# A linear-attention and feed-forward kernel: GpSimd's queue, not ScalarE's, asks for the load of w

## The chip, the core and the metric

The kernel runs on one core of a Trainium2 chip. The metric is the device time of one execution in microseconds (us); less is better. A core has five engines with a queue of instructions each: PE (TensorE, matrix products), DVE (VectorE), ACT (ScalarE), POOL (GpSimd) and SP (SyncE). In this kernel SP computes nothing: it issues DMAs, the transfers between the device's memory and the on-chip memory, and waits. "ACTq" or "SPq" in a profile is such an issue on that engine's queue.

## The reference

The first part is a linear attention with a decaying state, for 4 batches, 8 heads, 768 steps and a head size of 48. The second part is a feed-forward block with a gated softmax and a normalisation, from 384 to 1024 and back, over 3072 rows.

```python
for t in range(S):
    kt, vt, rt = (k[:, :, t], v[:, :, t], r[:, :, t])
    cur = np.einsum('bhd,bhe->bhde', u[None] * kt, vt)
    y[:, :, t] = np.einsum('bhd,bhde->bhe', rt, state + cur)
    state = w[None, :, :, None] * state + np.einsum('bhd,bhe->bhde', kt, vt)
...
h = x @ w_in
sm = e / (np.sum(e, axis=-1, keepdims=True) + 1e-09)
solu = h * sm
ln = (solu - mu) / np.sqrt(var + 1e-06) * g_ln
return (ln @ w_out).astype(np.float32)
```

Here `x` is y with its heads side by side, and `e` is exp(h - max h). w is small: 8 heads by 48 numbers, 1.5 KB. Each number is the decay of one row of the state.

## The kernel before

The 768 steps are cut into 6 chunks of 128 for each of the 4 batches: 24 units of (batch, chunk), chunk by chunk, so that a batch's next unit comes four units later. A unit's scores are computed as a product of decayed r and decayed k, and the state is carried from chunk to chunk inside the tiles that hold v. Behind each unit's attention follows its share of the feed-forward block: a product with w_in (L951), exponential and normalisation, and a product with w_out (L1061, L1106). The units overlap: a unit's second product comes several units behind its attention.

The order is written out by hand. `manual_schedule` (L459) keeps each engine's instructions in the order of the code, so an instruction that waits holds back everything behind it on its engine. A second path, `general_path`, runs only when a check on the data at the end asks for it, and it isn't taken here.

The start is what the change touches:

- ACT's queue issues two loads: w into `wq` (L493), then u into one row of `u_bc` (L496). ACT's first table load waits for u.
- SP's queue issues k and r of unit 0 (L475), the first piece of w_in (L524), k and r of unit 1, v of unit 0 (L480), the second piece of w_in, and so on (L594 to L608). Loads share eight semaphores in turn, so from the second piece of w_in on, each load is issued only after the load that last used its semaphore has landed.
- DVE clears the padding of `wq`, of five k tiles and five r tiles (L494 to L499), two banks of PSUM (L504), and sets one column of the table `tab` (L634).
- POOL makes `ident`, the identity for transposes, by `make_identity` (L611), a row of ones (L613), clears padding of the six v tiles (L623), and makes the masks (L671 to L676) and `ones` (L710).
- PE runs three products on `ident` whose result isn't used (`spin(3)`, L621), then transposes `wq` into `wd_ps` (L636), then spreads u over 128 partitions (`u_ps`, L638).

Then DVE clips `wd_ps` into `pw` (L643) and makes the powers of w by repeated squaring (L648, L649), and from them `tab` (L654), which doubles its filled part at each of seven steps. PE turns the table into `kdec` (L664). POOL computes `wide` from it (L1200), then `rku`, the product of k, u and r (L734, L735), and `kp`, the decayed k (L721). DVE sums rku to `own` (L739), ACT writes own on the diagonal of the score tile (L749), DVE copies the scores over it (L827), and PE makes unit 0's y (L858). The later units repeat this.

```python
wq = const.tile([HP, 2, P], F32, name="wq")
...
nc.tensor.transpose(wd_ps, wq.rearrange("a q d -> a (q d)"), ident[0:HP, 0:HP])
...
nc.gpsimd.tensor_tensor(out=wide.rearrange("p (a q) -> p a q", q=2)[P : P + D, :, q],
                        in0=back[rows, :, 0], in1=pw[rows, 0, 0], op=ALU.mult)
```

HP is 4, P is 64. In `wq` a row holds two heads of 48 numbers, each padded to 64.

Of the kernel before, what the change touches and what calls it, by code (L numbers as in the profile page):

```python
# [399 lines left out]
def direct_path(  # L400
# [29 lines left out]
    nc = tc.nc  # L430
    B, H, S, D = r.shape
# [53 lines left out]
    wq = const.tile([HP, 2, P], F32, name="wq")  # L485
# [4 lines left out]
    w_out_sb = const.tile([128, KF, dm], F32, name="w_out_sb")  # L490
    decays = const.tile([128, HP], F32, name="decays")

    nc.scalar.dma_start(out=wq[:, :, 0:D], in_=w.rearrange("(a q) d -> a q d", q=2))  # L493
    nc.vector.memset(wq[:, :, D:], 1.0)  # L494
    u_row = u_bc[0:1].rearrange("p h d -> p (h d)")
    nc.scalar.dma_start(out=u_row, in_=u.rearrange("h d -> (h d)").unsqueeze(0))  # L496
# [143 lines left out]
    for vt in vts:  # L640
        nc.scalar.activation(out=vt[:, 1].rearrange("p h x -> p (h x)"),
                             in_=ident[:, 0:1].to_broadcast([128, H * P]), func=ACT.Copy, scale=0.0)
# [916 lines left out]
def kernel(tc: tile.TileContext, *args):  # L1559

    with tc.tile_pool(name="flag", bufs=1) as pool:
        bad = direct_path(tc, pool, *args)
        value = tc.nc.values_load(bad, min_val=0, max_val=1)
        with tc.If(value != 0):
            general_path(tc, *args)
# [30 lines left out]
```

## Time and profile before

| what | value |
|---|---|
| median of 3 runs | 325.61 us (325.03 to 327.12) |
| the profiled execution: its own time | 326.14 us |
| its span, first to last instruction | 324.4 us |
| mean granted TensorE clock | 0.998 |
| w's issue on ACT's queue | starts 0.79 us, takes 1.25 us |
| u's issue on ACT's queue | starts 2.08 us, takes 0.27 us |
| wd_ps, the transpose of w | starts 4.34 us |
| first rku on POOL | starts 8.42 us |

Times in the profile count from the start of the span. Durations below come from the one profiled execution. The page gives each engine's busy time and the chain of work that ended last, followed back from the last instruction. The view of waits says which engine stood still, and what ended that. The timeline lists instructions in order of time; a bracket gives the idle time before one, and what released it. The DMA view counts packets by queue: queue 1 is SP's, queue 10 is ACT's.

### The profile page before, as it was taken

The numbers are of one execution on the slowest core, as the hardware profiler recorded it, in microseconds if no ns is written. First come the engines' busy times: TensorE is split into PE (matmuls) and PEld (weight loads), VectorE is DVE, ScalarE is ACT, GpSimd is POOL, SyncE is SP. The second block draws the span as 40 slices with busy tenths as digits, with TensorE's granted clock in tenths as the row PEclk, the third lists the DMA queues.
The fourth block names the chain that finished last, engine by engine and source line by source line (L and its number), as shares of the span: only waits on it lengthen the run. The fifth ranks groups of instructions, "written<-read, shape, count | busy, mean of one in ns | idle before, by whom it ended". The sixth has DMA issues, their size and how long they took to land.

```text
span 324.4 us, 9658 instructions
## 1 busy us (share of the span) xinstructions
PE 310.6 (96%) x3909; PEld 216.8 (67%) x3909; DVE 254.2 (78%) x434; ACT 244.0 (75%) x414; POOL 219.8 (68%) x237
## 2 busy tenths in 40 slices
PE   6889999999999999999999999999999999999993
PEld 4766565555556457668678668668668667769992
DVE  7796999998887979999779678997579675385471
ACT  4875888888469888868968969959958949957420
POOL 3989778799999999999999999979044020131000
PEclk9999999999999999999999999999999999999999
DMA  8999999579999999986998999987893473674611
GB/s 166 244 257 210 205 225 184 79 140 156 192 168 173 179 173 146 165 176 114 169 204 169 182 209 183 212 207 102 190 186 67 100 180 86 143 164 87 178 61 61
DMA packets 165780, 52.64 MB, mean 162 GB/s; under 512 B 158301, under 2 KB 161502, under 8 KB 165726
## 3 DMA queue, kind: packets, MB, share of 16 engines
q1 hardware_dynamic: 165712, 51.92, 83.0%
q8 instruction: 33, 0.54, 0.7%
q14 instruction: 21, 0.17, 0.2%
q10 hardware_dynamic: 14, 0.00, 0.0%
HBM read 26.75 MB, written 4.72 MB: 97 GB/s over the span
## 4 chain that ended last, share of the span: by engine, by line
PE 61%; POOL 14%; DVE 10%; issue 6%; ACT 4%; DMA 3%; POOLq 0%; DVEq 0%; ACTq 0%
PE h_ps L951 26%; PE o_ps L1106 23%; PE y_ps L875 4%; POOL rp L728 3%; POOL rku L734 3%; POOL big L754 3%; POOL kp L721 3%; PE at L819 2%; DMA rpad<-in_r_dram 2%; PE kv_ps L902 1%; POOL rku L735 1%; PE y_ps L858 1%; DVE big L832 1%; DMA wq<-in_w_dram 1%; DVE solu L963 1%
## 5 line engine op out<-in xcount | busy, mean ns | idle before, releaser
L951 PE MATMUL h_ps<-w_in_sb,xT 128*128 128x512 f32 x288 | 129.1, 597 | 0.0
L951 PEld LDWEIGHTS h_ps<-w_in_sb,xT 128*128 128x128 f32 x288 | 53.3, 190 | 59.5 <-issue 57.3
L1022 ACT COPY halves<-solu 128x2048 uint16<-128x2048 uint16 x24 | 45.5, 1895 | 1.3 <-DVE stats L961 1.1
L983 POOL TENSOR_SCALAR stats<-stats 128x2 f32<-128x2 f32 (+2 forms) x12 | 4.3, 361 | 48.7 <-ACT e L971 48.2
L1016 DVE COPY lnT<-halves 128x2048 uint16<-128x2048 uint16 x18 | 30.7, 1730 | 6.3 <-DMA halves<-halves 6.3
L956 ACT ACTIVATE e<-h_ps 128x1024 f32<-128x1024 f32 x24 | 24.5, 1020 | 14.5 <-PE h_ps L951 14.3
L1016 DVE COPY big<-halves 128x2048 uint16<-128x2048 uint16 x21 | 33.6, 1606 | 0.2
L721 POOL TENSOR_TENSOR kp<-kpad,kdec 128x512 f32<-128x512 f32 x24 | 32.6, 1360 | 0.7
L963 DVE SCALAR_TENSOR_TENSOR solu<-h_ps,stats,e 128x1024 f32<-128x1024 f32 x24 | 30.8, 1283 | 2.2
L754 POOL TENSOR_SCALAR_AFFINE_SELECT big<-own 64x512 f32<-64x512 f32 x40 | 29.1, 727 | 1.7
L735 POOL TENSOR_TENSOR rku<-rku,rpad 128x384 f32<-128x384 f32 x24 | 28.8, 1202 | 1.9
L832 DVE COPY_PREDICATED big<-later_half,at 64x512 f32<-64x512 uint32 x40 | 29.5, 738 | 0.7
L734 POOL TENSOR_TENSOR rku<-kpad,u_bc 128x384 f32<-128x384 f32 x24 | 29.8, 1242 | 0.1
L1106 PE MATMUL o_ps<-w_out_sb,ma 128*128 128x192 f32 x160 | 28.4, 329 | 0.1
L997 ACT ACTIVATE solu<-solu,stats 128x1024 f32<-128x1024 f32 x20 | 24.7, 1233 | 4.2 <-POOL stats L991 4.2
L941 POOL TENSOR_TENSOR vt<-vt,wide 48x384 f32<-48x384 f32 x16 | 20.2, 1276 | 10.2 <-DVE vt L938 9.5
L1106 PEld LDWEIGHTS o_ps<-w_out_sb,ma 128*128 128x128 f32 x160 | 26.0, 190 | 1.0 <-issue 0.6
L728 POOL TENSOR_TENSOR rp<-rpad,rdec 128x512 f32<-128x512 f32 x15 | 26.2, 1745 | 0.0
L961 DVE RECIPROCAL stats<-sums 128x1 f32<-128x1 f32 x24 | 3.8, 158 | 28.0 <-ACT e L956 27.8
L971 ACT ACTIVATE e<-solu,stats 128x1024 f32<-128x1024 f32 x20 | 22.9, 1145 | 1.4 <-DVE solu L963 1.1
L1061 PE MATMUL o_ps<-w_out_sb,lnT 128*128 128x384 f32 x64 | 21.6, 491 | 0.0
L875 PE MATMUL y_ps<-big,vt 128*32 128x64 f32 (+1 forms) x1280 | 20.7, 220 | 0.5 <-issue 0.5
(148 smaller groups left out, 607.8 us busy)
## 6 DMA issues: line engine op xcount, KB each, us to landing
raw<-in_moe_w_out_dram SPq DMA_DIRECT2D x16, 384.0 KB, 4.1
kpad<-in_k_dram SPq DMA_DIRECT2D x24, 192.0 KB, 5.0
rpad<-in_r_dram SPq DMA_DIRECT2D x24, 192.0 KB, 5.1
vt<-in_v_dram SPq DMA_DIRECT2D x40, 96.0 KB, 3.9
out_dram<-o SPq DMA_DIRECT2D x20, 192.0 KB, 3.7
raw<-in_moe_w_in_dram SPq DMA_DIRECT2D x7, 512.0 KB, 6.3
raw<-in_moe_w_in_dram SPq DMA_DIRECT2D x10, 256.0 KB, 3.6
vt<-in_v_dram SPq DMA_DIRECT2D x4, 192.0 KB, 5.9
```

The source lines that it names most:

```text
L721: nc.gpsimd.tensor_mul(X["kp"].rearrange("p h d -> p (h d)"), kpads[i % NLD].rearrange("p h d -> p (h d)"), kdec.rearrange("p a d -> p (a ...
L728: nc.gpsimd.tensor_mul(X["rp"].rearrange("p h d -> p (h d)"), rpads[i % NLD].rearrange("p h d -> p (h d)"), rdec.rearrange("p a d -> p (a ...
L734: engine.tensor_mul(rku, kpads[i % NLD][:, :, 0:D], u_bc)
L735: engine.tensor_mul(rku, rku, rpads[i % NLD][:, :, 0:D])
L754: nc.gpsimd.affine_select(out=G[rows, c].rearrange("p a q u -> p (a q) u"), in_=X["own"][rows].to_broadcast([U, H, U]), compare_op=ALU.is_ ...
L832: nc.vector.copy_predicated(X["G"][rows, c].rearrange("p a q u -> p q a u"), later_half[rows].unsqueeze(1).to_broadcast([U, 2, HP, U]), X[ ...
L875: nc.tensor.matmul(y_ps[ts(g, 32), j, ts(c, U)], vf[:, at : at + 32], X["G"][rows, c, h // 2, h % 2, :], start=(g not in opened), stop=las ...
L951: nc.tensor.matmul(h_ps[:, ts(n, NX)], X["xT"][:, j, :], w_in_sb[:, j, ts(n, NX)], start=(j == 0), stop=(j == KD - 1))
L963: nc.vector.scalar_tensor_tensor(out=solu, in0=X["h"], scalar=rs, in1=X["e"], op0=ALU.mult, op1=ALU.mult, accum_out=tot)
L1016: nc.vector.tensor_copy(out=words.bitcast(U16).rearrange("p n (t o) -> p o n t", o=2), in_=turned)
L1022: nc.scalar.copy(out=both.rearrange("p (o n) -> p o n", o=2), in_=split(X["solu"]))
L1106: nc.tensor.matmul(dst, rows[:, f], weights[:, f], start=(start and f == 0), stop=(f == KH - 1), skip_group_check=True)
```

## The change

The load of w is asked for on GpSimd's queue instead of ScalarE's. Nothing else in the code differs.

```diff
-    nc.scalar.dma_start(out=wq[:, :, 0:D], in_=w.rearrange("(a q) d -> a q d", q=2))
+    nc.gpsimd.dma_start(out=wq[:, :, 0:D], in_=w.rearrange("(a q) d -> a q d", q=2))
     nc.vector.memset(wq[:, :, D:], 1.0)
     u_row = u_bc[0:1].rearrange("p h d -> p (h d)")
     nc.scalar.dma_start(out=u_row, in_=u.rearrange("h d -> (h d)").unsqueeze(0))
```

In the built programs the load leaves the head of ACT's queue, where u's load becomes the first instruction, and stands on POOL's queue directly before the memset that begins `ident`. PE's transpose of w waits for a semaphore of POOL's DMAs. Since w no longer takes one of the eight semaphores of the other loads, the second piece of w_in, which waited for w's landing before, is issued without a wait; the third load of k waits for u instead of the first k, and the third load of r for the first k instead of u. All other instructions and waits stand as before.

## The prediction

> **What bounds the kernel now.** I read the page first, for shares.
>
> ```profile
> PE 310.6 (96%) x3909; PEld 216.8 (67%) x3909; DVE 254.2 (78%) x434; ACT 244.0 (75%) x414; POOL 219.8 (68%) x237
> PE 61%; POOL 14%; DVE 10%; issue 6%; ACT 4%; DMA 3%; POOLq 0%; DVEq 0%; ACTq 0%
> ```
>
> PE is busy for 310.6 of 324.4 us, so only 13.8 us are idle. The windows view puts 2.69 of them in the first 8 us (5.31 busy of 8.00), 2.36 in 8 to 23 us, 1.88 in 23 to 139 and 6.9 after. A change in the first microseconds counts in full only if all later work hangs on it, so the second view is the chain of waits over the first 15 us (start, length, what):
>
> ```profile
> 0.79 3.42 DMA wq<-in_w_dram
> 4.21 0.14 issue
> 4.34 0.25 PE wd_ps L636
> 4.59 0.02 issue
> 4.62 0.16 DVE pw L643
> ...
> 7.04 0.70 DVE tab L654
> ...
> 8.42 1.02 POOL rku L734
> ```
>
> The chain begins with the very load that is moved. It takes 3.42 us from issue to landing, at 4.21. Then PE turns the four rows of w, DVE makes the tables of powers (4.62 to 7.74), and POOL starts rku at 8.42; from there POOL, DVE, ACT and PE follow each other without a visible wait for a load until 34 us. So w's landing sets the start of everything, and a microsecond here should reach the end nearly whole. The third view, the waits of the first 9 us, says how closely (waited us, times, longest):
>
> ```profile
> POOL wide L1200 <- DVE tab L654: 4.0, 1, 4.0
> PE spin L619 <- POOL ident masks.py:199: 1.4, 1, 1.4
> PE wd_ps L636 <- DMA wq<-in_w_dram: 1.3, 1, 1.3
> DVE pw L643 <- PE wd_ps L636: 1.0, 1, 1.0
> ```
>
> PE waits 1.3 us for w and DVE 1.0 us for PE; POOL has 4.0 us of nothing before its first dependent instruction. The last view is the timeline (start, length, engine):
>
> ```profile
> 0.78 0.20 POOL masks.py:197 MEMSET ident<- 128x128 f32 x1 [0.29 <-POOLq L1583]
> 0.79 1.25 ACTq L493 DMA_DIRECT2D wq<-in_w_dram  x1
> 1.41 1.65 PE L619 MATMUL spin<-ident 128*128 128x128 f32 x6 [1.41 <-POOL ident masks.py:199]
> 2.08 0.27 ACTq L496 DMA_DIRECT2D u_bc<-in_u_dram  x1
> 3.60 0.06 DVE L634 MEMSET tab<- 128x4 f32 x1
> 3.80 0.10 POOL L710 MEMSET ones<- 128x1 f32 x1
> 7.89 0.45 POOL L1200 TENSOR_TENSOR wide<-tab,pw 48x4 f32<-48x4 f32 x2 [3.99 <-DVE tab L654]
> ```
>
> POOL's own start-up work ends at 3.90. PE's spins end at 3.06. The small table memset, which wd_ps stands behind through a wait on DVE, ends at 3.66. So PE could have transposed w about 0.7 us sooner.
>
> The DMA answer for 2.8 to 3.2 us has 12 packets on queue 10, ACT's:
>
> ```profile
> q1 hardware_dynamic: 501, 0.09, 118.8%
> q10 hardware_dynamic: 12, 0.00, 2.4%
> ```
>
> w's data thus moved at about 2.8 to 3.1, inside the flood of queue 1 (SP's loads of k, r and the weights), and about 1.1 us more went by until it counted as landed.
>
> **What the Trainium skill says.** "DMA: Bandwidth & Descriptors", section "SWDGE vs HWDGE vs iDMA": a DMA asked for by GpSimd has its descriptors written by that engine's own cores, those of ScalarE and SyncE by hardware. No DMA from POOL is in this trace, so it shows nothing of this. The same page, "Why a DMA increments its semaphore by 16 and not by 1": the hardware path completes on only the engines it uses, the software path on all 16. The trace fits the first half: 12 packets are 8 rows of w and 4 completions. The same page, "Issuing engines are not separate DMA queues": all issuers share the same 16 engines. The trace agrees: w's packets lie among SP's. "SBUF — State Buffer", "Who interferes with whom": a VectorE instruction in a two-port mode can stop GpSimd from writing descriptors. VectorE runs memsets from 0.85 to 3.66 here, 0.17 us for 128 columns; no run here shows whether any holds the port.
>
> **The change part by part.**
>
> *ACT loses one issue.* 1.25 us at 0.79 goes, and u's issue moves from 2.08 to about 0.79. As first on its queue I give it the same 1.25 us, so it ends near 2.04 instead of 2.35, and u lands 0.3 us earlier than 4.37, when ACT's table load, which waits for u, started. The product on u runs behind wd_ps on PE and ends at 6.07, its copy at 6.58, and rku needs it at 8.42: 1.8 us of cover. Gain on the path: 0.
>
> *SP's queue.* w's completion no longer stands before the second load of w_in. In the trace that load is issued at 7.12, because the vt load before it held the queue from 3.90 to 7.08; w landed at 4.21. Gain 0. SP's other waits keep their distance. The first copies of k and r have to wait for u and k instead, both long there.
>
> *POOL gains one issue ahead of ident.* Nothing in this trace prices the hold H. The skill's DMA page, "Latency and other measured facts", states about 1 us to the first byte for the software path against about 0.6 for the hardware path, so my estimate is H = 1.1 us; the bounds are 0.1 (only a hand-over) and about 5 (a slow first use, which I can't exclude). Behind it stand 20 instructions of start-up, ident first. All move by H: they end at 3.90 + 1.1 = 5.0, and are needed at 7.77 by wide. Cover is 3.87 us, cost 0. But PE waits for ident: the spins end at 3.06 + H = 4.16, while wd_ps starts at 4.34. Cover is 1.28 us, cost 0 at H = 1.1, and H - 1.28 above that.
>
> *w's landing.* Issue 0.78, plus H 1.1, plus 0.77 from the end of issue to the first packet (as ACT's: 2.04 to 2.81), plus 0.3 for the packets, plus 1.1 to the landing: 4.05. For completions from all 16 engines, of which each is full of SP's packets by then, and for descriptors that must be fetched, I add 0.4 as a guess between 0 and 1. That is 4.45, against 4.21: +0.24. From the bounds: H = 0.1 and no extra give 3.05, where the 3.66 memset takes over, with a gain of about 0.65 on wd_ps (4.34 to 3.7); H = 1.5 and 1.0 extra give 5.45, a loss of 1.2; H = 5 gives about 8.3, a loss of 4.1.
>
> *Sum.* 0 + 0 + 0 + 0.24: the profiled execution's span goes from 324.4 to 324.6, its own time from 326.14 to 326.4. That execution is 0.5 above the median of 325.61, inside the runs' spread of 325.03 to 327.12. On the median I forecast 325.61 + 0.24, rounded up to 325.9.
>
> **Rivals.** *Earlier w.* ACT's issue took 1.25 us while SP issued at the same time; if a handover to POOL is quick, w lands by 3.6 and wd_ps starts at 3.7. For it: PE and DVE sit idle (1.3 and 1.0 us). Against it: ident also sits behind the issue, so the gain is at most min(0.65, 1.28 - H). Time: 325.0. *Slow software issue.* The first DMA that POOL makes holds its queue for several us, or its descriptors are starved by DVE's memsets. Place: POOL at 0.78. It costs nothing on wd_ps up to a landing of 4.21, then 1 us for 1 us. For 1% (3.26 us) w must land at 7.5, 6.7 us after the request; H = 4.5 does it, since 0.78 + 4.5 + 2.2 = 7.5. Against it: memsets end at 3.66, so starving alone gives a landing of about 3.66 + 1.1 + 2.2 = 7.0, +2.8. The two together, or a slower first use: 330. For it: no software-path DMA is in the trace, so nothing bounds it from above. *Re-timing.* A shift of tenths moves POOL against DVE in 66 to 121 us, where the chain lies on POOL and the same product takes 1.27 or 2.29 us; the three runs before, which also differ in such phases, span 2.1 us, so I give it ±2 in most cases, centred on 325.9. *Absorbed.* PE's idle 0.91 us near 20.7, put down to issue, could take up tenths. Then 325.6, which is no different from my forecast to a measurement.
>
> **How the numbers follow.** Forecast with absorption 0.45 (all within 1%). Earlier w 0.20 (0.17 within, 0.03 faster with re-timing). Slow issue 0.28 (0.24 over 1% slower, 0.04 within). Re-timing alone 0.07 (0.03 faster, 0.02 within, 0.02 slower). That makes faster 0.06, same 0.68, slower 0.26; 1% is about what a measurement of this kernel can tell from no change. Range: below 324.6 lies about 0.1 (earlier w with luck, re-timing), above 330.6 about 0.1 (hold over 5 us). The forecast's own range is 325.0 to 327.2.
>
> **What would show it.** Right: POOL's ident memset starts near 1.9, the spins near 2.5, w lands at 4.2 to 4.9, wd_ps starts at 4.3 to 5.0, rku at 8.4 to 9.1, and all later chain entries are shifted by the same amount. Earlier w: wd_ps below 4.2. Slow issue: ident or w's landing after 5.5, with PE waiting on one of them, and rku after 9.7. Wrong altogether: wd_ps within 0.5 us of 4.34 and an end more than 3 us away, so that the shift was multiplied later; or q10 still carrying 14 packets.

## The result, and the profile after

| | before | changed |
|---|---|---|
| median of 22 runs each | 325.84 us | 326.82 us |
| ratio, 95% interval | 1 | 1.0028 (1.0014 to 1.0041) |
| profiled execution: own time, span | 326.14, 324.4 us | 326.34, 324.6 us |
| w landed | 4.21 us | 5.24 us |
| wd_ps starts | 4.34 us | 5.37 us |
| first rku starts | 8.42 us | 9.45 us |

The kernel became slower by 0.28% (0.14 to 0.41%), some 0.9 us: within 1%, and on the slow side. The chain of waits of the changed kernel over the first 15 us (start, length, what) is to be laid beside the one of before:

```profile
0.69 0.76 issue
1.45 3.79 DMA wq<-in_w_dram
5.24 0.14 issue
5.37 0.25 PE wd_ps L636
5.62 0.02 issue
5.64 0.16 DVE pw L643
...
8.07 0.70 DVE tab L654
...
9.45 1.01 POOL rku L734
```

Link for link it is the old chain, 1.03 us later. The whole difference arises before wd_ps: the request becomes visible at 1.45 instead of 0.79, and takes 3.79 instead of 3.42 us to land. The timeline (start, length, engine) shows the rest of the start:

```profile
0.80 0.51 ACTq L496 DMA_DIRECT2D u_bc<-in_u_dram  x1
1.45 0.81 POOL L493 DMA_DIRECT2D wq<-in_w_dram  x1 [0.95 <-POOLq L1583]
2.14 1.28 ACT L639 ACT_TABLE_LOAD   x1 [2.14 <-DMA u_bc<-in_u_dram]
2.26 0.22 POOL masks.py:197 MEMSET ident<- 128x128 f32 x1
2.90 1.65 PE L619 MATMUL spin<-ident 128*128 128x128 f32 x6 [2.90 <-POOL ident masks.py:199]
5.30 0.10 POOL L710 MEMSET ones<- 128x1 f32 x1
8.92 0.45 POOL L1200 TENSOR_TENSOR wide<-tab,pw 48x4 f32<-48x4 f32 x2 [3.52 <-DVE tab L654]
```

POOL is held from 0.78 to 2.26: 0.67 us before the request shows, then 0.81 us of it. All its start-up work is 1.5 us later and still ends 3.52 us before it is needed. PE's spins end at 4.55, 0.82 us before wd_ps, so the hold isn't what PE waits for last:

```profile
PE wd_ps L636 <- DMA wq<-in_w_dram: 0.8, 1, 0.8
```

u, now first on ACT's queue, landed by 2.14 instead of 4.37, and nothing gains by it. The DMA view of the first 6 us has w on a queue of its own:

```profile
q0 software_dynamic: 32, 0.00, 0.6%
q10 hardware_dynamic: 2, 0.00, 0.1%
```

The 32 packets are 4 with w's rows (384 bytes each), 12 of 8 bytes, and 16 of 4 bytes. The last fit one completion for each of the 16 engines, as the Trainium skill says of this path ("DMA: Bandwidth & Descriptors", section "Why a DMA increments its semaphore by 16 and not by 1"). By the packets' own times the first moved at 3.78 and the last at 4.20.

Further on, the shift shrinks. PE's products with w_in (L951) of unit 0 and, on the last line, of unit 1, which the view cuts off at 36 us; the kernel before, then the changed one:

```profile
21.61 0.30 PE L858 MATMUL y_ps<-big,vt 128*32 128x128 f32 x2 [0.91 <-issue]
23.32 5.42 PE L951 MATMUL h_ps<-w_in_sb,xT 128*128 128x512 f32 x12
33.50 2.84 PE L951 MATMUL h_ps<-w_in_sb,xT 128*128 128x512 f32 x6
```

```profile
20.85 1.09 PE L858 MATMUL y_ps<-big,vt 128*32 128x128 f32 x26 [0.16 <-DVE big L827]
23.34 5.81 PE L951 MATMUL h_ps<-w_in_sb,xT 128*128 128x512 f32 x12
34.15 2.41 PE L951 MATMUL h_ps<-w_in_sb,xT 128*128 128x512 f32 x5
```

The idle 0.91 us of PE near 21 is gone, so the product starts only 0.02 us later; but DVE and POOL, which turn w_in's pieces into usable weights, still run 1.0 us late, and PE waits for them inside it (5.81 against 5.42). From 34 us the products stand 0.65 us later, and 0.7 to 0.8 us later up to 200 us. Near 205 to 215 us several of the profiled executions jump by -1.0 to +0.3 us against that of before, without a wait that the views name; so the medians, not single spans, are used for times.

### The profile page after: what moved, and what is told of

Read it like the earlier page. It is cut to its first block, busy times and chain, and to the rows that moved or that the text cites. A ratio compares the mean times of both kernels' runs of the same rounds, so it can differ in the third digit from the quotient of the medians.

```text
span 324.6 us, 9659 instructions
## 1 busy us (share of the span) xinstructions
PE 311.9 (96%) x3909; PEld 217.5 (67%) x3909; DVE 255.0 (79%) x434; ACT 244.2 (75%) x414; POOL 221.0 (68%) x238
## 4 chain that ended last, share of the span: by engine, by line
PE 54%; POOL 16%; DVE 16%; issue 7%; ACT 4%; DMA 1%; POOLq 0%; DVEq 0%; ACTq 0%
PE o_ps L1106 23%; PE h_ps L951 21%; PE y_ps L875 4%; POOL rp L728 3%; POOL rku L734 3%; POOL big L754 3%; POOL kp L721 3%; DVE big L832 2%; PE at L819 2%; DVE ma L552 2%; POOL rku L735 2%; DVE solu L963 2%; PE kv_ps L902 1%; DMA wq<-in_w_dram 1%; DVE vt L923 1%
## 5 line engine op out<-in xcount | busy, mean ns | idle before, releaser
L951 PE MATMUL h_ps<-w_in_sb,xT 128*128 128x512 f32 x288 | 129.3, 598 | 0.1
L951 PEld LDWEIGHTS h_ps<-w_in_sb,xT 128*128 128x128 f32 x288 | 53.2, 190 | 60.0 <-issue 56.8
L875 PE MATMUL y_ps<-big,vt 128*32 128x64 f32 (+1 forms) x1280 | 20.7, 220 | 0.2 <-issue 0.2
```

Source lines behind the costliest of these rows:

```text
L875: nc.tensor.matmul(y_ps[ts(g, 32), j, ts(c, U)], vf[:, at : at + 32], X["G"][rows, c, h // 2, h % 2, :], start=(g not in opened), stop=las ...
L951: nc.tensor.matmul(h_ps[:, ts(n, NX)], X["xT"][:, j, :], w_in_sb[:, j, ts(n, NX)], start=(j == 0), stop=(j == KD - 1))
```

## The experiments

Theory L: the end follows the landing of w. Rival H: POOL's hold does it. In every diff the base is named; ratios are to the kernel before, with 95% intervals.

**The hold alone** (base: before; the extra copy of w is read by nobody).

```diff
+    again = const.tile([HP, 2, P], F32, name="again")
+    nc.gpsimd.dma_start(out=again[:, :, 0:D], in_=w.rearrange("(a q) d -> a q d", q=2))
     nc.scalar.dma_start(out=wq[:, :, 0:D], in_=w.rearrange("(a q) d -> a q d", q=2))
```

> w stays on ACT's queue; POOL's queue asks, at its head, for a second copy of w that nothing reads. So POOL is held as in the changed kernel, and w's own load is as before. Theory L (w's late landing is the whole loss, 1 us for 1 us): ident and the spins move by about 1.5 us, the spins end near 4.55, w lands near 4.2, so wd_ps starts at 4.5 to 4.7 and the first rku at 8.6 to 8.8; time +0.2 us, ratio about 1.0006. Rival H (the loss comes from POOL's hold, which delays ident and all of POOL's start): wd_ps at 5.3 and rku at 9.4 as in the changed kernel, ratio about 1.003.

Ratio 0.9994 (0.9977 to 1.001). Its timeline:

```profile
2.26 0.22 POOL masks.py:197 MEMSET ident<- 128x128 f32 x1
4.48 0.26 PE L638 MATMUL wd_ps<-ident,wq 4*128 4x4 f32 x1
8.59 1.02 POOL L736 TENSOR_TENSOR rku<-kpad,u_bc 128x384 f32<-128x384 f32 x1
```

The full hold is there, ident at 2.26, and costs wd_ps 0.14 us and the end nothing that can be measured. H falls as the cause of the loss. A small share of it isn't excluded: the interval reaches 0.3 us. Nor is this the hold alone, for the copy's packets move among the others, and u landed at 5.32 instead of 4.37. In the profiled execution PE's products with w_in stand 0.3 to 0.4 us late from 33 to 200 us, against 0.65 to 0.8 us in the changed kernel.

**The request behind ident** (base: changed).

```diff
-    nc.gpsimd.dma_start(out=wq[:, :, 0:D], in_=w.rearrange("(a q) d -> a q d", q=2))
...
     nc.gpsimd.memset(ones_row, 1.0)
+    nc.gpsimd.dma_start(out=wq[:, :, 0:D], in_=w.rearrange("(a q) d -> a q d", q=2))
```

> w on POOL's queue, but asked for behind ident and the row of ones, so PE's spins start as before and w is asked for later. Theory L: ident starts at 0.78 again, the spins end near 3.1, the request slips by 0.5 to 0.7 us, w lands at 5.7 to 6.0, rku starts at 9.9 to 10.2; time 0.5 to 0.7 us above the changed kernel, ratio to before 1.0045 to 1.005. Rival H (POOL's hold of ident is the loss): wd_ps back near 4.4 and the time as before, ratio 1.000.

Ratio 1.0029 (1.0014 to 1.0044). The chain has

```profile
1.51 0.16 issue
1.67 3.52 DMA wq<-in_w_dram
```

with ident at 0.79 again. I expected a later landing and was wrong: the request shows at 1.67, only 0.22 us later than at the head of the queue, since all but 0.16 us of the 0.76 us without a recorded instruction ahead of it are gone. That they pass under ident's work is my reading; no run tests it. w landed at 5.19, and the time is that of the changed kernel. With ident on time and w late, the loss stays: that is L again.

**w asked for twice on POOL** (base: changed; a copy that nobody reads goes first), and **w late on ACT** (base: before; no POOL DMA).

```diff
+    again = const.tile([HP, 2, P], F32, name="again")
+    nc.gpsimd.dma_start(out=again[:, :, 0:D], in_=w.rearrange("(a q) d -> a q d", q=2))
     nc.gpsimd.dma_start(out=wq[:, :, 0:D], in_=w.rearrange("(a q) d -> a q d", q=2))
```

> The changed kernel, with a copy of w that nothing reads asked for on POOL's queue ahead of w. Theory L (the end follows w's landing): the second request is issued 0.8 us later, w lands near 6.0, rku starts near 10.3; time 0.5 to 0.8 us above the changed kernel, ratio to before 1.0045 to 1.0055. Rival N (the loss is a fixed price of using POOL's DMA queue at all, at the start or the end): ratio as for the changed kernel, 1.003.

```diff
-    nc.scalar.dma_start(out=wq[:, :, 0:D], in_=w.rearrange("(a q) d -> a q d", q=2))
...
     nc.scalar.dma_start(out=u_row, in_=u.rearrange("h d -> (h d)").unsqueeze(0))
+    again = const.tile([HP, 2, P], F32, name="again")
+    nc.scalar.dma_start(out=again[:, :, 0:D], in_=w.rearrange("(a q) d -> a q d", q=2))
+    nc.scalar.dma_start(out=wq[:, :, 0:D], in_=w.rearrange("(a q) d -> a q d", q=2))
```

> No DMA on POOL's queue at all: ACT's queue asks for u, then for a copy of w that nothing reads, then for w. Theory L (the end follows w's landing, whoever asks): the request is issued near 2.5, w lands at 5.0 to 5.5, wd_ps starts near 5.2 to 5.6, rku near 9.4, ratio 1.0025 to 1.0035. Rival N (the price is that of POOL's queue): ratio 1.000 to 1.001 in spite of a late rku.

Their chains, POOL first:

```profile
2.28 4.51 DMA wq<-in_w_dram
11.02 1.02 POOL rku L736
```

```profile
2.16 4.58 DMA wq<-in_w_dram
10.96 1.01 POOL rku L736
```

w landed at 6.79 and 6.74, rku starts 2.60 and 2.54 us late, and the ratios are 1.0071 (1.0044 to 1.0099) and 1.006 (1.0038 to 1.0081). Both landed some 0.8 and 1.5 us later than I had reckoned, and the sizes of the loss were missed with that; the comparison stands. A price of POOL's queue as such (rival N) isn't the cause: the kernel without a POOL DMA loses as much, within the intervals, when w is as late, and the kernel with the hold alone, which has a POOL DMA, loses at most 0.1%.

**Why does it land late?** Two causes for the 1.52 us between the end of POOL's issue and w's first packet were tried, in one execution each (base: changed; only w's packets are read, not the time). First DVE's early memsets:

```diff
-    for i in range(NLD):
+    for i in range(1):
         nc.vector.memset(kpads[i][:, :, D:P], 0.0)
         nc.vector.memset(rpads[i][:, :, D:P], 0.0)
...
-    for ps in banks:
-        nc.vector.memset(ps, 0.0)
...
+    for ps in banks:
+        nc.vector.memset(ps, 0.0)
+    for i in range(1, NLD):
+        nc.vector.memset(kpads[i][:, :, D:P], 0.0)
+        nc.vector.memset(rpads[i][:, :, D:P], 0.0)
     kdec = const.tile([128, HP, 128], F32, name="kdec")
```

> The changed kernel, but DVE clears only the padding of w, of the first k tile and of the first r tile at the start; the other eight clears and the two banks come behind the tables. Only w's packets on POOL's DMA queue are read here, not the time, since 2.5 us of DVE work are put where DVE is needed. In the changed kernel POOL's issue ends at 2.26 and w's first packet moves at 3.78, 1.52 us later. Theory F (the path of a POOL request is that long by itself): first packet again at 3.6 to 3.9. Rival D (DVE's memsets, which run to 3.67, hold the descriptors up): first packet at 2.8 to 3.1.

Then SP's flood:

```diff
+    gate = const.tile([1, D], F32, name="gate")
+    nc.sync.dma_start(out=gate, in_=wq[0:1, 0, 0:D])
     load(0, "kr")
```

> The changed kernel, with one more DMA of 192 bytes at the head of SP's queue, which copies one row of the landed w: so SP's loads of k, r, v and the weights begin only after w has landed. The time must be several us longer and isn't read. Theory F (path): w's first packet still at 3.6 to 3.9; only the packets and the landing get quicker (in the changed kernel 0.43 us of packets, then 1.03 us to the landing). Rival Q (SP's flood holds w's first packet back): first packet at 2.6 to 3.1, with the landing by 3.6.

Chains, memsets moved first, then the quiet queue:

```profile
1.45 3.79 DMA wq<-in_w_dram
```

```profile
1.45 1.92 DMA wq<-in_w_dram
```

Without the memsets the first packet moves at 3.43 instead of 3.78, and w lands at 5.24 as before: they aren't the cause. Without the flood it moves at 2.83, 0.57 us after the issue's end, and w lands at 3.37 instead of 5.24. Of the 3.79 us, 1.87 are SP's other loads. Rival Q holds.

**Is it POOL's path, or the moment?** (base: before, ACT's two loads swapped.)

```diff
-    nc.scalar.dma_start(out=wq[:, :, 0:D], in_=w.rearrange("(a q) d -> a q d", q=2))
...
     nc.scalar.dma_start(out=u_row, in_=u.rearrange("h d -> (h d)").unsqueeze(0))
+    nc.scalar.dma_start(out=wq[:, :, 0:D], in_=w.rearrange("(a q) d -> a q d", q=2))
```

> No DMA on POOL's queue: the kernel before with ACT's two loads swapped, u first, then w. In the runs so far w's landing after the end of its issue was 2.17 us for an issue that ended at 2.04 (ACT), 2.98 for 2.26 (POOL), 2.71 for 2.48 (POOL), 3.94 for 2.80 (ACT) and 3.92 for 2.87 (POOL). Theory T (the delay goes by the moment at which the request meets SP's flood of loads, whichever queue asks): w's issue runs from about 1.35 to 2.1 and lands at 4.9 to 5.3, rku at 9.1 to 9.5, ratio 1.002 to 1.003, as in the changed kernel. Rival P (a request of POOL's queue takes longer by itself, and ACT's needs about 2.2 us): w lands by 4.4, rku by 8.7, ratio 1.000 to 1.001.

Ratio 1.0024 (1.0006 to 1.0042). Its chain:

```profile
1.36 3.81 DMA wq<-in_w_dram
9.38 1.02 POOL rku L734
```

ACT's issue of w now ends at 2.13, 0.09 us later than before, and w lands at 5.17, 0.96 us later: nearly the same landing, rku and loss as in the changed kernel, without POOL. So POOL's path isn't needed for the delay. The landings gather at 4.2 (issue ended at 2.04, ACT's queue only), 5.2 (2.13 to 2.48, both queues) and 6.8 us (2.80 and 2.87, both queues).

What sets these steps stays open. The moment of the request is my reading, but the swap also puts w behind u, and in every kernel in which w landed near 5.2 or later u was asked for first; no run separates the two. And u shows that the moment isn't all. Its request ended at 2.35 in the kernel before and at 2.37 with the hold alone, where a copy of w was asked for on POOL's queue; ACT's table load, which waits for u, began at

```profile
4.37 1.28 ACT L639 ACT_TABLE_LOAD   x1 [4.37 <-DMA u_bc<-in_u_dram]
```

```profile
5.32 1.28 ACT L641 ACT_TABLE_LOAD   x1 [5.32 <-DMA u_bc<-in_u_dram]
```

So u landed 0.95 us apart for requests made at nearly the same moment, and in the kernel before it landed earlier than w did from an earlier request in the swap.

**Can an earlier w win?** (base: before; w first on SP's queue; then also with the memset of L634, and the two lines that make `tab`, moved up behind the clear of `wq`; then, without that memset moved, with v of unit 1 loaded ahead of the third piece of w_in.)

```diff
-    nc.scalar.dma_start(out=wq[:, :, 0:D], in_=w.rearrange("(a q) d -> a q d", q=2))
+    nc.sync.dma_start(out=wq[:, :, 0:D], in_=w.rearrange("(a q) d -> a q d", q=2))
```

> w asked for by SP's queue, as its first load; ACT asks for u alone. Theory L (the end follows the start of the tables): w lands at 2.7 to 3.3, wd_ps is then held by the table memset and starts near 3.7, rku near 7.8, time 0.5 to 0.65 us below before, ratio 0.998. Rival A (a gain at the start is absorbed later, where PE is full): rku near 7.8 and ratio 1.000. Rival S (SP's loads of k, r and the weights all slip by w's issue of 0.5 to 1.25 us, and they bind): wd_ps near 3.7 but the first DVE product on tr_ps or the first at later than before, ratio 1.001 or above.

```diff
     nc.vector.memset(wq[:, :, D:], 1.0)
+    tab = const.tile([128, 2, HP, T], F32, name="tab")
+    back, fore = tab[:, 0], tab[:, 1]
+    nc.vector.memset(back[:, :, T - 1 : T], 1.0)
...
-    tab = const.tile([128, 2, HP, T], F32, name="tab")
-    back, fore = tab[:, 0], tab[:, 1]
     pw = const.tile([128, 2, 8, HP], F32, name="pw")
-    nc.vector.memset(back[:, :, T - 1 : T], 1.0)
```

> As with w first on SP's queue, and the memset of the table's column is moved to the head of DVE's queue. Theory L: wd_ps is then held by the spins (end near 3.1) or w's landing (2.7 to 3.3) and starts at 3.1 to 3.4, rku at 7.2 to 7.5, time 0.9 to 1.2 us below before, ratio 0.9965. Rival A: ratio 1.000 with rku near 7.4. Rival S: another wait (k's or r's load, u's copy) holds the first rku at 7.8 or later, ratio 0.998 or above.

```diff
-    load_weights(2)
     load(1, "v")
+    load_weights(2)
```

> As with w first on SP's queue, and v of unit 1 is loaded ahead of the third piece of w_in instead of behind it. With w first, the second unit's y waited 0.60 us for that load and the weight conversions 1.9 us for pieces of w_in. Theory S (SP's stream of loads is a second bound, some tenths of a us behind the chain from w): the wait of y for v goes and y starts near 18.3, but the pieces of w_in still come late, so PE's first product of unit 1 with w_in starts no earlier than 0.3 to 0.7 us before the kernel before has it (33.50); ratio 0.997 to 1.000. Rival A (early gains are lost later, where PE is full, whatever SP's stream does): that product 1 us or more earlier and still ratio 1.000 or above.

Ratios 1.0016 (0.9997 to 1.0036), 0.9997 (0.9979 to 1.0016) and 1.0035 (1.0018 to 1.0052). In the first, wd_ps starts at 2.98 and rku at 7.34, 1.08 us early. The memset of L634 begins only later, so wd_ps doesn't wait for it, as I had assumed:

```profile
2.98 0.26 PE L636 MATMUL wd_ps<-ident,wq 4*128 4x4 f32 x1
3.60 0.06 DVE L634 MEMSET tab<- 128x4 f32 x1
```

Then PE and ACT wait for loads of w_in and v, as they don't in the kernel before:

```profile
ACT lows L537 <- DMA raw<-in_moe_w_in_dram: 1.9, 2, 1.2
PE y_ps L858 <- DMA vt<-in_v_dram: 0.6, 1, 0.6
```

With v earlier, the second line goes and the first grows, and PE stops inside unit 0's product for weights that aren't ready:

```profile
ACT lows L537 <- DMA raw<-in_moe_w_in_dram: 3.5, 4, 2.1
```

```profile
26.26 1.13 PE L951 MATMUL h_ps<-w_in_sb,xT 128*128 128x512 f32 x2 [0.67 <-POOL w_in_sb L560]
```

That product begins 1.5 us early, and unit 1's, at 33.71, is 0.21 us late. This kernel is slower than the one before, above the 0.997 to 1.000 that I had expected. With the memset moved it is alike: unit 0's product begins 2.0 us early, PE waits for weights inside it, and unit 3's product is 0.2 us late.

w at the head of SP's queue delays all of SP's loads: k's first packet moves at 2.79 instead of 1.92. That stream is a second bound, just behind the chain from w. Rival S holds in these two kernels, and my own expectation of a gain fell. In the first kernel it is only part of the answer: in its profiled execution unit 1's product starts at 32.92, still 0.58 us early, and later ones are 0.35 to 0.4 us early from 93 to 190 us, yet the medians show no gain. Rival A, that such a lead is lost later, isn't excluded there. None of these kernels beats the one before by a measurable amount.

## Why the prediction was right, point by point

It forecast 325.9 us, little slower, within 1%; measured were 326.82, inside the range, and a ratio of 1.0028. The mechanism (w's landing is the head of the chain, and the rest is covered) was right; one size was off, and the forecast owes its place in the range in part to the range's 2.2 us, since the shift was about 0.9 us where 0.24 had been reckoned. Of the signs that the prediction gave for being right, one held, that all later entries of the chain shift alike. The times all came later than it had set them: ident 2.26, spins 2.90, landing 5.24, wd_ps 5.37, rku 9.45. Its signs of a slow issue, a landing after 5.5 and rku after 9.7, weren't reached either.

- *ACT loses one issue*: gain 0, as said. u's issue took 0.51 us, not my 1.25, and u landed by 2.14.
- *SP's queue*: gain 0, as said. The second piece of w_in was issued at 6.95, against 7.12.
- *POOL's hold H*: estimated at 1.1, measured 1.48 us. The estimate rested on a price for the first byte, which is another time: w's first packet moved 1.38 us after its request showed with SP's loads held back and 2.33 us under SP's loads. The hold's cost on wd_ps, "H - 1.28 above that", would be 0.2; the hold alone gave 0.14. On POOL's own work it cost 0.
- *w's landing* is the term that was mis-sized: 4.45 reckoned, 5.24 measured. The issue ended at 2.26 instead of 1.88 (+0.38). From there to the first packet I had ACT's 0.77 and 0.4 for the path; it took 1.52 (+0.35). The packets took 0.43 instead of 0.3, the landing 1.03 instead of 1.1. Together +0.79, so that +0.24 became +1.03 us. The fault lay in taking ACT's 0.77 as a property of the path: it was that of one request, issued by 2.04, 0.12 us after SP's first packet had moved. With ACT's loads swapped, ACT's own request, issued by 2.13, took 1.71 us.
- *A microsecond reaches the end nearly whole*: +1.03 us at rku gave about 0.9 at the end, +2.5 gave 2.0 to 2.3.
- *Absorbed*: in part. PE's idle 0.91 us near 20.7 took up the shift for PE's first product, but not for DVE and POOL.
- *Slow software issue*: its place was right, its price wasn't reached. The part of it that blamed DVE's memsets is refuted for the landing.
- *Earlier w*: it didn't come, and its price of 325.0 was wrong as well. Its floor of 3.66, the memset of L634, doesn't exist: with w first on SP's queue wd_ps started at 2.98. But with rku 1.08 us early the ratio was still 1.0016, in part because SP's loads bind next. I had read "without a visible wait for a load until 34 us" as room; it was nearly a tie.

## What to carry to other kernels

In this kernel a small load at the head of a chain was priced by how its request met the bulk loads, not by the queue that asked: with two loads of one queue swapped, 0.09 us at the request went with 0.96 us at the landing. So look at what stands around such a request, not only at what its issue costs. Where a chain shows no wait for a load, ask how far behind it the loads land before counting on a gain from a faster chain. Here a late start passed on to the end; an early one met the next bound.

## What the runs showed that I had not expected

- Ahead of POOL's first request at the head of its queue there are 0.76 us without a recorded instruction. Behind ident's work, 0.16 us of such time is left, and a second request begins 0.01 us after the first has ended.
- ACT's issue of w took 1.25 us as its first load and 0.77 us as its second; u's took 0.51 as the first and 0.27 as the second.
- With SP's loads held back POOL's request of w took 1.92 us from issue to landing, against 3.79 under SP's loads.
